# Folding the mirror images of x on VectorE, a first stage in 64x64 tiles, and a special row by copies

## The chip, the cores and the metric

The kernel runs on one core of a Trainium2 chip. The core has TensorE (PE, matrix products, reads SBUF and writes PSUM), VectorE (DVE), ScalarE (ACT) and GpSimd (POOL) for elementwise work, and DMA queues that SyncE (SP), ScalarE and GpSimd start. Each engine runs its own instructions in the order in which the program gives them. The metric is the device time of one execution in microseconds (us). Three runs of the kernel before took 132.18, 133.13 and 133.68 us; their median is 133.13 us.

## The reference, cut to what matters

```python
x = A_x                                              # 1 x 2048 x 512, fp32
g = _sigmoid((x * gate_w).sum(-1, keepdims=True))    # one gate per row of x
X = rfft2(x) * (w_r + 1j * w_i)                      # a: a filter in the 2-D spectrum
a = irfft2(X, (2048, 512))
K = 2 Re sum_n C_n exp(A_n dt * pos)                 # b: a long convolution per channel
b = irfft(rfft(x_t, 4096) * rfft(K, 4096))[:2048] + x * D_skip
return g * a + (1 - g) * b
```

The branch `a` is the bulk of the work: a 2-D Fourier transform of x, a product with the filter, and the transform back. For `b` the kernel uses that with these inputs the convolution's kernel is a constant for each channel, so that `b` is a running sum of x along the rows, times a factor per channel, plus x times another one; a count of channels for which this holds guards a general path, which these inputs do not take. Both are mixed by the gate.

## The kernel before, in words

All data is fp32. The 2048 rows are split as 32 x 64 and the transform along them is made in two stages with twiddles inside the second; the 512 channels are ordered so that channel t and its mirror images 511-t, 255-t, 256+t stand at the same place of four groups of 128.

The stages, by the letters of the schedule (`PLAN`), with their lines in the kernel before:

- `A` loads x into the tile `GI` (its first 64 blocks are called `X`) in ten parts, 4 MB in all. `X` loads a second, transposed copy of x into `XT` (four parts of 1 MB) for the running sums. `r` loads parameters, `l` the filter's weights (each of them over a block of `X` that the first stage has read), `R` constants.
- `C` (L233) is the first stage along the rows: for each of 8 groups k, 8 products of a 128x128 block of `X` with the constant `s1`, also 128x128. The sums and differences of mirror images are part of that constant. A product in fp32 shows as two records in the profile. `c` copies the result from PSUM to `E1` (L238, on ScalarE; one group, `f`, on VectorE).
- `D` (L248) is the transform along the channels, 8 products for each of 8 groups u; `E` (L253, ScalarE) copies it out. `P` (L269) is the second stage along the rows for 9 groups u = 0 to 8 (the last is half as large).
- `d` (L275, ScalarE) copies a part of P's result, `Z` (L290, L291, VectorE, four instructions for each u) combines row f with row -f, `W` and `U` (L311, L316, L317, VectorE) multiply by the filter, `p` (L321) is a DMA started by GpSimd that adds one half of the product to the other in SBUF.
- `g` (L328, L329, GpSimd) makes sums and differences, `I` (L338, L339, L341) goes back along the channels. One channel frequency does not fit the pattern of the other 127; it stands on partition 127, and `I` corrects for it with two narrow products (L341, 32 rows by 64 columns of the array) for each pair of full ones. `i` (L346, ScalarE) copies the result back to `GI`. The weights of that frequency come through a transpose on TensorE (`J`, L465) and small DMAs on SP (`L`, L305).
- `B` (L357, L358, L363) and the transposes `T` (L367, VectorE) go back along the rows; `Q` (L476) is the last stage; `q` (L481, VectorE) adds the other branch and starts the output's DMA (L482).
- Beside it: `m` (L436, VectorE) makes the running sums, `s` (L439, ScalarE) scales them; for the channels' groups 0 and 1 `e` and `o` (L442, VectorE) add them to the scaled x, for 2 and 3 `v`, `w` (L445, ScalarE) scale x and `M` (L449) adds by DMA. `H` (L453, GpSimd) multiplies by the gate; `G` makes the gate (L375 on TensorE, L378 on ScalarE), `K` (L397, VectorE) and `k` (L403, ScalarE) put the gate into the constants of the last stage. Small sums (`N`, L409 to L423) go to the guard.

PSUM is four tiles of two banks each, `banks[i]`; SBUF work tiles are `blk(i)` and `pairs[i]`. Nothing but `PLAN` sets the order: its words are issued from left to right, the number behind a letter is the group, the ones behind the points are the tiles it uses, and each engine sees its own instructions in that order. Semaphores between the engines are put in from the tiles that are read and written.

## Time and profile before

| what | number |
|---|---|
| median of three runs | 133.13 us |
| the profiled execution, by the device's time | 134.16 us |
| its span, first to last instruction | 132.4 us |
| outside the span in that execution | 1.76 us |
| TensorE busy | 117.2 us (89%) |
| VectorE busy | 82.2 us (62%) |
| ScalarE busy | 51.2 us (39%) |
| GpSimd busy | 56.2 us (42%) |
| moved by DMA | 29.85 MB, 226 GB/s over the span |
| mean granted TensorE clock | 0.979 |

In the profile's groups a row has the line, the engine, the operation, output and inputs, the shapes, the count, then busy time and the mean ns of one instruction, then the time for which the engine stood idle just before them and what ended it. A mean contains the latency of the pipeline, so where instructions follow closely the distance of two starts is the better price of one. In the chain of waits and in the timeline a row has start and length in us.

### The profile page before, as it was taken

To read this page: it belongs to the slowest core of one execution; us is meant where nothing else is said; L and a number is where in the kernel's file an instruction comes from. 1 tells how busy PE (TensorE), PEld (TensorE's weight loads), DVE (VectorE), ACT (ScalarE), POOL (GpSimd) and SP (SyncE) were. 2 spreads that over 40 slices of the span, in tenths; PEclk is the share of its full clock that TensorE was granted. 3 is DMA by queue.
4 is the path that set the end of the run, shared out by engine and by line. 5 is a ranking of instruction groups with operands and counts; after the bars stand their busy time and mean duration, and the time that the engine had idled before them with its cause. 6 is when DMAs were issued, how large, how long until landed. Compare 5 with 4: busy or idle time off the path is not lost.

```text
span 132.4 us, 2360 instructions
## 1 busy us (share of the span) xinstructions
PE 117.2 (89%) x944; PEld 95.5 (72%) x944; DVE 82.2 (62%) x101; ACT 51.2 (39%) x63; POOL 56.2 (42%) x49
## 2 busy tenths in 40 slices
PE   0599998999979999989999999999999999999700
PEld 0599997999879998858736766777655339999600
DVE  0031036078299999788770099999999573677610
ACT  3033635444267542313164113349679970000000
POOL 0000000001040840586798919499949999300000
PEclk9999999999999999999999999999999999999965
DMA  2999989996869789998667769990969600099660
GB/s 83 349 396 384 392 309 272 389 389 136 314 195 223 253 238 276 274 386 174 126 130 147 141 144 316 295 335 10 191 131 198 124 5 7 9 368 396 267 245 5
DMA packets 10643, 29.85 MB, mean 226 GB/s; under 512 B 1818, under 2 KB 2938, under 8 KB 10366
## 3 DMA queue, kind: packets, MB, share of 16 engines
q1 hardware_dynamic: 8606, 22.99, 48.4%
q0 software_dynamic: 1872, 6.55, 25.9%
q8 instruction: 9, 0.15, 0.4%
q10 hardware_dynamic: 144, 0.07, 0.4%
q14 instruction: 12, 0.10, 0.2%
HBM read 18.82 MB, written 4.21 MB: 174 GB/s over the span
## 4 chain that ended last, share of the span: by engine, by line
PE 69%; DMA 15%; DVE 7%; POOL 2%; issue 2%; ACT 1%
PE ps L233 13%; PE ps L476 12%; PE ps L357 11%; PE ps L338 9%; PE ps L341 8%; DMA blk<-blk 8%; PE ps L339 5%; PE ps L269 4%; DMA short<-in_prms_dram 3%; DMA GI<-in_x_dram 3%; PE ps L248 3%; PE ps L375 3%; DVE ps L290 2%; DVE ps L291 2%; DVE blk L316 1%
## 5 line engine op out<-in xcount | busy, mean ns | idle before, releaser
L233 PE MATMUL ps<-s,GI 128*128 128x128 f32 x128 | 17.4, 307 | 4.9 <-DMA GI<-in_x_dram 4.9
L453 POOL TENSOR_TENSOR XT<-XT,hg 128x1024 f32<-128x1024 f32 x8 | 20.9, 3038 | 0.0
L233 PEld LDWEIGHTS ps<-s,GI 128*128 128x128 f32 x128 | 17.2, 222 | 4.8 <-DMA s<-in_c_s_dram 4.8
L346 ACT COPY GI<-ps 128x1024 f32<-128x1024 f32 (+1 forms) x9 | 8.7, 964 | 24.2 <-PE ps L341 24.2
L328 POOL TENSOR_TENSOR blk<-blk 128x512 f32<-128x512 f32 (+1 forms) x9 | 13.0, 1443 | 11.6 <-DMA blk<-blk 11.2
L248 PE MATMUL ps<-dfw,E 128*128 128x128 f32 x128 | 15.6, 277 | 2.2 <-DVE blk L317 1.6
L248 PEld LDWEIGHTS ps<-dfw,E 128*128 128x128 f32 x128 | 14.8, 192 | 2.9 <-DVE blk L317 2.0
L338 PE MATMUL ps<-dbw,blk 128*128 128x128 f32 x68 | 16.3, 322 | 0.6 <-POOL blk L329 0.6
L269 PE MATMUL ps<-s2e,blk 128*128 128x128 f32 x136 | 16.8, 277 | 0.0
L269 PEld LDWEIGHTS ps<-s2e,blk 128*128 128x128 f32 x136 | 15.8, 192 | 1.2 <-issue 0.8
L357 PE MATMUL ps<-GI,s2p 128*64 128x512 f32 (+1 forms) x64 | 15.7, 583 | 0.0
L436 DVE TENSOR_TENSOR_SCAN run<-XT 128x1024 f32<-128x1024 f32 x4 | 11.2, 2803 | 6.7 <-DMA XT<-in_xt_dram 6.7
L476 PE MATMUL ps<-blk,E 128*128 128x128 f32 x128 | 15.3, 282 | 0.0
L476 PEld LDWEIGHTS ps<-blk,E 128*128 128x128 f32 x128 | 15.2, 196 | 0.1
L341 PE MATMUL ps<-last,blk 32*64 32x128 f32 x136 | 14.8, 293 | 0.0
L338 PEld LDWEIGHTS ps<-dbw,blk 128*128 128x128 f32 x68 | 10.1, 188 | 5.8 <-issue 5.0
L415 POOL TENSOR_TENSOR few<-few 128x4 f32<-128x4 f32 x1 | 0.2, 202 | 31.5 <-ACT few L412 31.5
L339 PE MATMUL ps<-dbw,blk 128*128 128x128 f32 x68 | 13.1, 275 | 0.0
L481 DVE TENSOR_TENSOR blk<-ps,XT 128x1024 f32<-128x1024 f32 x8 | 9.6, 1222 | 5.6 <-PE ps L476 2.8
L329 POOL TENSOR_TENSOR blk<-blk 128x512 f32<-128x512 f32 (+1 forms) x9 | 12.6, 1404 | 0.0
L238 ACT COPY E<-ps 128x1024 f32<-128x1024 f32 x7 | 7.1, 1012 | 13.7 <-PE ps L233 13.7
L311 DVE TENSOR_TENSOR blk<-ps,GI 128x1024 f32<-128x1024 f32 (+1 forms) x9 | 10.5, 1164 | 3.1 <-PE ps L341 1.8
(51 smaller groups left out, 142.7 us busy)
## 6 DMA issues: line engine op xcount, KB each, us to landing
XT<-in_xt_dram SPq DMA_DIRECT2D x4, 1024.0 KB, 6.6
GI<-in_w_dram SPq DMA_DIRECT2D x8, 512.0 KB, 3.9
blk<-blk POOLq DMA_DIRECT2D x8, 512.0 KB, 5.7
out_dram<-blk SPq DMA_DIRECT2D x8, 512.0 KB, 3.3
GI<-in_x_dram SPq DMA_DIRECT2D x6, 512.0 KB
XT<-run POOLq DMA_DIRECT2D x4, 512.0 KB, 5.9
GI<-in_x_dram SPq DMA_DIRECT2D x4, 256.0 KB, 5.4
hg<-gd SPq DMA_DIRECT2D x1, 1024.0 KB
```

The costliest lines, as they stand in the source:

```text
L233: T.matmul(p[:, u, :, j], X[:, 8 * k + 4 * u + j], s1, start=True, stop=True)
L248: T.matmul(p[:, n], E1[:, 8 * u + n], dfw[:, n % 4], start=True, stop=True)
L269: T.matmul(p[:, h, :, o, 64 * v:64 * v + 64], t_["e2", u % 8][:, 4 * v + 2 * h + o], st[:, ::-1] if h else st, start=True, stop=True)
L328: G.tensor_tensor(gt[:, :, :, 0], t[:, 0:4:3], t[:, 1:3], op=ALU.add)
L329: G.tensor_tensor(gt[:, ::-1, :, 1], t[:, 0:4:3], t[:, 1:3], op=ALU.subtract)
L338: T.matmul(p[:, v, 2 * h + 1], gt[:, h, m + v], dbw[:, h, 1], start=True, stop=True)
L339: T.matmul(p[:, v, 2 * h], gt[:, h, v], dbw[:, h, 0], start=True, stop=False)
L341: T.matmul(p[64 * c:64 * c + 64, v, 2 * h], px[:, c ^ h, h, v], dbl[:, h], start=False, stop=True, tile_position=(96, 64 * c))
L357: T.matmul(p[64 * s:64 * s + 64, u, :16 * n], s2p[:, 0, g], GI[:, 32 * s:32 * s + n, tt], start=True, stop=s == 1, tile_position=(0, 64 * s))
L436: V.tensor_tensor_scan(run[:, q % 2, 1:1025], XT[:, 0, q], XT[:, 1, q], 0.0, op0=ALU.add, op1=ALU.add)
L453: G.tensor_tensor(o, o, hg[:, 1024 * (k % 2):1024 * (k % 2) + 1024], op=ALU.mult)
L476: T.matmul(p[:, u, :, j], E4[:, b // 16, b % 16, :, u], t_["q", b // 8][:, 8 * u + b % 8].rearrange("p q a -> p (q a)"), start=True, stop= ...
```

## The change

Four things are done. First, `S` on VectorE makes the sums and the differences of x's mirror images out of `X` into work tiles while x comes in: for each group k one sum and one difference of 128x512 elements, and for the two groups that are loaded in halves two of each of 128x256. The host hands x over in another order, so that a block holds two mirror images on its two halves of partitions. Second, `C` works on these in tiles of 64 rows by 64 columns of the array: 32 products for each k, with a 64x64 constant and 64 columns each, in place of 8 of 128x128x128; the two row halves write to the two banks of a PSUM tile. All eight copies `c` are on ScalarE. Third, the special frequency: `h` on ScalarE copies its product row (32 partitions are copied, of which the last is kept) into the operand of the second transform; L341 and its constant are gone, so that `I` is 8 full products for each u. The row's weights come apart from the others (`wl`), by small DMAs on ScalarE's queue, and the large loads of weights fill 127 partitions. Fourth, the combinations `g` are split in two halves: `g` (the half without the special row) on GpSimd for all u, the other one as `x` on GpSimd for u = 0, 8, 1, 2 and as `y` on VectorE for u = 5, 6, 3, 7, 4.

The `PLAN` is written anew. Besides the moves above, the running sums of channel groups 0 and 1 are now added as those of 2 and 3 are, by ScalarE's scaling and a DMA (`v`, `w`, `M`), so `e` and `o` do not occur any more, and all ten parts of x are loaded ahead of everything else on SP.

```diff
 PLAN = """
-R0 A4 C3.0 A7 C6.1 r0.0 A3 c3 C2.0 r1.1 N0 A5 R3 J0 A6 C4.2 R8 A9 A8 c6 c2 C5.0 c4 f5 A1 C7.1 c7 A2 C1.0 R4 c1 A0 C0.1
...
+A2 S1.0 A0 A1 S0.1 A7 R0 S6.2 A9 A8 S7.3 C1.0 c1 A3 S2.0 C0.1 C6.0 A5 S4.1 C7.2 c0 c7 c6 C2.1 C4.2 c2 A4 S3.2 A6 c4
...
+        def S_(k, i):
+            f = t_["fo", k] = blk(i).rearrange("p (o b t) -> p o b t", o=2, t=P)
+            n = 2 if k in (0, 7) else 4
+            for b in range(0, 4, n):
+                v = X[:, 8 * k + 2 * b:8 * k + 2 * b + 2 * n].rearrange("p (b u) t -> p u b t", u=2)
+                V.tensor_tensor(f[:, 0, b:b + n], v[:, 0], v[:, 1], op=ALU.add)
+                V.tensor_tensor(f[:, 1, b:b + n], v[:, 0], v[:, 1], op=ALU.subtract)
+
         def C_(k, i):
-            p = t_["pc", k] = bank(i).rearrange("p u (n b) -> p u n b", b=4)
-            for u in range(2):
-                for j in range(4):
-                    T.matmul(p[:, u, :, j], X[:, 8 * k + 4 * u + j], s1, start=True, stop=True)
+            p = bank(i)
+            t_["pc", k] = p.rearrange("p g (n b) -> p g n b", b=4)
+            p = p.rearrange("p g (m o c b) -> p g m o c b", o=2, c=2, b=4)
+            for b in range(4):
+                for o in range(2):
+                    for g in range(2):
+                        for h in range(2):
+                            gs, hs_ = slice(64 * g, 64 * g + 64), slice(64 * h, 64 * h + 64)
+                            T.matmul(p[hs_, g, :, o, :, b], t_["fo", k][gs, o, b, hs_], s1[gs], start=True, stop=True, tile_position=(64 * g, 64 * h))
...
+        def load_h(k):
+            main = GI[P - 1:P, 0:64].rearrange("p (u n o) t -> p u n o t", n=4, o=2)[:, :, :, k]
+            nc.scalar.dma_start(main, hT[0:8] if k == 0 else wl[0:4096].rearrange("(o u n t) -> o u n t", o=1, u=8, n=4))
+            main = wtile(8)[P - 1:P, :, :, k].rearrange("p r a k -> p (r a) k")
+            nc.scalar.dma_start(main, hT[8:9, :, :64] if k == 0 else wl[4096:].rearrange("(o n t) -> o n t", o=1, n=4))
...
-        def g_a(u, i):
+        def h_a(u, i):
             n = nrow(u)
-            gt = t_["gt", u] = blk(i)[:, 0:8 * n].rearrange("p (h m c k) -> p h m c k", h=2, c=2, k=64)
-
-            t = t_["t", u][:, 0].rearrange("p x a (m k) -> p (x a) m k", k=64)
-            G.tensor_tensor(gt[:, :, :, 0], t[:, 0:4:3], t[:, 1:3], op=ALU.add)
-            G.tensor_tensor(gt[:, ::-1, :, 1], t[:, 0:4:3], t[:, 1:3], op=ALU.subtract)
+            t_["gt", u] = blk(i)[:, 0:8 * n].rearrange("p (h o v c k) -> p h o v c k", h=2, o=2, c=2, k=64)
+            t = t_["t", u][96:P, 0, :, :, 0:n].rearrange("p x a (v k) -> p x a v k", k=64)
+            for h in range(2):
+                S.copy(t_["gt", u][96:P, h, 0].rearrange("p v c k -> p c v k"), t[:, ::-1, 1] if h else t[:, :, 0])
+
+        def g_a(u, o, E):
+            n = nrow(u)
+            r = P - 1 + o
+            gt = t_["gt", u][:r, :, o]
+
+            t = t_["t", u][:r, 0, :, :, o * n:o * n + n].rearrange("p x a (v k) -> p (x a) v k", k=64)
+            E.tensor_tensor(gt[:, :, :, 0], t[:, 0:4:3], t[:, 1:3], op=ALU.add)
+            E.tensor_tensor(gt[:, ::-1, :, 1], t[:, 0:4:3], t[:, 1:3], op=ALU.subtract)
 
         def I_(u, i):
...
-            for v in range(m):
-                for h in range(2):
-                    T.matmul(p[:, v, 2 * h + 1], gt[:, h, m + v], dbw[:, h, 1], start=True, stop=True)
-                    T.matmul(p[:, v, 2 * h], gt[:, h, v], dbw[:, h, 0], start=True, stop=False)
-                    for c in range(2):
-                        T.matmul(p[64 * c:64 * c + 64, v, 2 * h], px[:, c ^ h, h, v], dbl[:, h], start=False, stop=True, tile_position=(96, 64 * c))
+            gt = t_["gt", u].rearrange("p h o v c k -> p h o v (c k)")
+            for o in (1, 0):
+                for v in range(nrow(u) // 64):
+                    for h in range(2):
+                        T.matmul(p[:, v, 2 * h + o], gt[:, h, o, v], dbw[:, h, o], start=True, stop=True)
...
-            "W": W_, "U": U_, "p": p_a, "g": g_a, "I": I_, "i": i_a,
+            "W": W_, "U": U_, "p": p_a, "h": h_a, "g": lambda u: g_a(u, 1, G), "x": lambda u: g_a(u, 0, G), "y": lambda u: g_a(u, 0, V), "I": I_, "i": i_a,
```

Three places show what this moves. A row has the line, the operation, output and inputs with buffer numbers, the shape of one and the count.

VectorE at the start of the program, before: `few` holds small numbers, `short` are loaded parameters, `E` is `E1`, `run` the running sum, `ps` PSUM.

```order
L409 TENSOR_REDUCE few<-short_96 128x4
L409 TENSOR_REDUCE few<-short_97 128x4
L459 TENSOR_TENSOR few<-few 128x9x2
L460 TENSOR_TENSOR few<-few 128x9
L461 TENSOR_TENSOR few<-few 128x9
L240 COPY E_69<-ps_58 128x2x128x4
L436 SCALAR_TENSOR_TENSOR run<-XT 128x1024 x2
L290 TENSOR_TENSOR ps_59<-ps_59,short_96 128x2x128
```

The same place in the changed kernel, from the last folds on (L230, L231):

```order
L230 TENSOR_TENSOR blk_88<-GI 128x512
L231 TENSOR_TENSOR blk_88<-GI 128x512
L472 TENSOR_TENSOR few<-few 128x9x2
L473 TENSOR_TENSOR few<-few 128x9
L474 TENSOR_TENSOR few<-few 128x9
L449 SCALAR_TENSOR_TENSOR run<-XT 128x1024
L422 TENSOR_REDUCE few<-short_97 128x4
L422 TENSOR_REDUCE few<-short_96 128x4
L449 SCALAR_TENSOR_TENSOR run<-XT 128x1024
L299 TENSOR_TENSOR ps_58<-ps_58,short_96 128x2x128
```

Twenty folds stand ahead of all else; the copy of `E1` is gone; the two reductions stand between the two running sums, and the first `Z` (L299) still follows the second running sum.

TensorE where the transform back along the channels begins, before: one `I` for u = 6 and the `P` behind it (`blk_88` is the combined operand, `blk_95` the product with the special row).

```order
L338 MATMUL ps_58<-dbw,blk_88 128x128
L339 MATMUL ps_58<-dbw,blk_88 128x128
L341 MATMUL ps_58<-last,blk_95 64x128 x2
L338 MATMUL ps_58<-dbw,blk_88 128x128
L339 MATMUL ps_58<-dbw,blk_88 128x128
L341 MATMUL ps_58<-last,blk_95 64x128 x2
L269 MATMUL ps_59<-s2e,blk_90 128x2x64 x8
```

TensorE around the first `I` (L354) in the changed kernel: `P` is L278, `D` is L257, the gate's count L443.

```order
L278 MATMUL ps_59<-s2e,blk_90 128x2x64 x8
L354 MATMUL ps_60<-dbw,blk_89 128x128 x4
L278 MATMUL ps_61<-s2e,blk_90 128x2x64 x8
L354 MATMUL ps_58<-dbw,blk_89 128x128 x8
L354 MATMUL ps_60<-dbw,blk_88 128x128 x8
L354 MATMUL ps_59<-dbw,blk_88 128x128 x8
L443 MATMUL ps_58<-few 1x1 x4
```

The narrow products are gone, and all `I` but the short one stand behind the last `P`.

VectorE after the last multiplication by the filter, before: `share` (L442) and the running sums of groups 2 and 3.

```order
L317 SCALAR_TENSOR_TENSOR blk_92<-ps_59,GI 128x256
L442 SCALAR_TENSOR_TENSOR XT<-XT,few,run 128x1024 x2
L436 SCALAR_TENSOR_TENSOR run<-XT 128x1024
L442 SCALAR_TENSOR_TENSOR XT<-XT,few,run 128x1024 x2
L436 SCALAR_TENSOR_TENSOR run<-XT 128x1024
L397 TENSOR_TENSOR short_96<-short_96,blk_95 128x512
```

The same place in the changed kernel; L345 and L346 are `y`, L446 the guard's count, L410 the constants' gate.

```order
L326 SCALAR_TENSOR_TENSOR blk_93<-ps_61,GI 128x512
L345 TENSOR_TENSOR blk_89<-blk_94 127x2x2x64
L346 TENSOR_TENSOR blk_89<-blk_94 127x2x2x64
L449 SCALAR_TENSOR_TENSOR run<-XT 128x1024
L345 TENSOR_TENSOR blk_89<-blk_91 127x2x2x64
L346 TENSOR_TENSOR blk_89<-blk_91 127x2x2x64
L345 TENSOR_TENSOR blk_88<-blk_90 127x2x2x64
L346 TENSOR_TENSOR blk_88<-blk_90 127x2x2x64
L446 CAST count<-ps_58 1x1
L345 TENSOR_TENSOR blk_88<-blk_95 127x2x2x64
L346 TENSOR_TENSOR blk_88<-blk_95 127x2x2x64
L410 TENSOR_TENSOR short_98<-short_98,blk_92 128x512
```

The four `share` instructions are gone, and five pairs of combinations, four of them shown, stand between the running sum, the count and the first product with the gate.

More of the change, by code (lines that the diff above doesn't have):

```diff
@@ L167, in body @@
     X = GI[:, 0:64]
-    s1 = work.tile([P, P], F32, name="s1")
+    s1 = work.tile([P, 64], F32, name="s1")
     few = work.tile([P, 72 + 36 + 24 + 17], F32, name="few")
@@ L178, in body @@
     dbw = work.tile([P, 2, 2, P], F32, name="dbw")
-    last = work.tile([P, 4, P], F32, name="last")
-    hT, dbl = last[:9], last[96:P, 0:2]
+    hT = work.tile([9, 4, P], F32, name="hT")
     gws = work.tile([P, 4, 32], F32, name="gws")
```

45 lines of the change are left out of this document (18 added, 27 removed).

## The prediction

> **What bounds the kernel now.** I read the page first, then the chain of waits, then the groups of instructions with shapes apart, then timelines of single engines. On the page I look at shares, at the slices and at the DMA queues:
>
> ```profile
> PE 117.2 (89%) x944; PEld 95.5 (72%) x944; DVE 82.2 (62%) x101; ACT 51.2 (39%) x63; POOL 56.2 (42%) x49
> ...
> PE   0599998999979999989999999999999999999700
> ...
> q0 software_dynamic: 1872, 6.55, 25.9%
> ```
>
> TensorE is busy from about 5 us to 125 us with next to no gap, so it bounds the whole; no other engine is above 62%. The chain in order of time (start, length, both us) gives the stages:
>
> ```profile
> 0.75 3.97 DMA GI<-in_x_dram
> ...
> 4.86 17.37 PE ps L233 x128
> 22.25 1.02 ACT E L238
> 23.31 3.84 PE ps L248 x32
> ...
> 36.12 0.60 DVE blk L316
> ...
> 72.45 0.42 PE ps L338 x2
> ...
> 73.45 0.42 PE ps L338 x2
> ...
> 93.84 1.00 PE ps L357 x3
> ...
> 109.58 15.29 PE ps L476 x128
> 124.89 1.23 DVE blk L481
> ```
>
> The first stage lasts until 22.2; D starts at 23.3; B starts at 93.8; B and Q take 31.1 us until 124.9; the last 7.5 us of the span of 132.4 are the last sum and the output's transfer. One set of I's (two full products, two narrow ones) costs 73.45 - 72.45 = 1.00 us, and there are 34 sets. The groups give the prices of single things:
>
> ```profile
> L248 PE MATMUL ps<-dfw,E 128*128 128x128 f32 x128 | 15.6, 277 | 2.2 <-DVE blk L317 1.6 <-ACT E L238 0.7
> L375 PE MATMUL ps<-XT,gws 128*32 128x512 f32 x32 | 3.6, 595 | 0.0
> L430 PE MATMUL ps<-few 128*1 128x1 f32 x8 | 0.3, 163 | 0.0
> L275 ACT COPY short<-ps 128x256 f32<-128x256 f32 x1 | 0.4, 373 | 0.0
> L321 POOL DMA_DIRECT2D blk<-blk x9 | 8.5, 945 | 8.2 <-DVE blk L317 8.2
> L328 POOL TENSOR_TENSOR blk<-blk 128x512 f32<-128x512 f32 x8 | 11.0, 1371 | 9.7 <-DMA blk<-blk 9.2 <-PE ps L375 0.3
> L453 POOL TENSOR_TENSOR XT<-XT,hg 128x1024 f32<-128x1024 f32 x8 | 20.9, 3038 | 0.0
> ```
>
> **What goes from TensorE.** A full product is two records of 15.6/128 = 0.122 us, 0.244 us. Without the narrow ones a set of I's is two full products, 0.49 us: 34 x (1.00 - 0.49) = 17.3 us less, if nothing else sets the pace of I.
>
> The first stage is 64 full products now; it becomes 256, each on a quarter of the array, with half the columns. How those run no row shows. The nearest is the gate's product L375, with four column tiles and 512 columns. Two rows of TensorE's timeline for the distance of D and P, and one that caught the first four records of L375:
>
> ```profile
> 45.17 1.95 PE L269 MATMUL ps<-s2e,blk 128*128 128x128 f32 x16
> 46.96 1.95 PE L248 MATMUL ps<-dfw,E 128*128 128x128 f32 x16
> ...
> 66.91 0.64 PE L375 MATMUL ps<-XT,gws 128*32 128x512 f32 x4
> ```
>
> One record of L375 takes 0.595 us, yet four fit in 0.64 us and all 32 cost 3.6/32 = 0.112 us each: four tiles run at once. For 64 columns in place of 512 that is an estimate of 0.014 us a record, 512 x 0.014 = 7.2 us for the stage. L430's smallest records, in a single tile, cost 0.3/8 = 0.038 us, which gives 19.2 us; a record as long as a full one, 0.122 us, gives 62 us. I take the low end, as L375 alone has four tiles at work, and keep the others as rivals.
>
> The Trainium skill, "TensorE: Matmul & The Clock Gate" (section "Wait — 56ns, not 53.3ns?"), has a floor of about 25 ns from one start to the next however few columns there are; by it the stage takes 512 x 0.025 = 12.8 us and the time is about 0.5 us more. L375's row speaks against it between tiles: its four records started within 0.64 - 0.595 = 0.045 us.
>
> **When the first stage can end.** If the tiles run at once, x's arrival sets it. One window of the trace (the last numbers are the DMA's share and GB/s), and two queue rows with the operand that waits:
>
> ```profile
> 0.00:13.24 13.24, 8.38 (x50) 8.42 (x51) 1.81 (x7) 3.31 (x3) 0.20 (x4) 1.00 0.83 303
> ...
> 13.07 0.71 SPq L207 DMA_DIRECT2D XT<-in_xt_dram  x1
> ...
> 21.18 2.29 DVE L436 TENSOR_TENSOR_SCAN run<-XT 128x1024 f32<-128x1024 f32 x1 [2.99 <-DMA XT<-in_xt_dram]
> ...
> 29.59 0.43 DVE L290 TENSOR_TENSOR ps<-ps,short 128x256 f32<-128x256 f32 x1
> ...
> 45.48 0.42 DVE L290 TENSOR_TENSOR ps<-ps,short 128x256 f32<-128x256 f32 x1
> ...
> 49.66 0.42 DVE L290 TENSOR_TENSOR ps<-ps,short 128x256 f32<-128x256 f32 x1
> ...
> 75.91 0.28 DVE L290 TENSOR_TENSOR ps<-ps,short 128x128 f32<-128x128 f32 x1
> ...
> 78.55 5.16 DVE L442 SCALAR_TENSOR_TENSOR XT<-XT,few,run 128x1024 f32<-128x1024 f32 x2
> ```
>
> 303 GB/s over 13.24 us are 4.01 MB, 0.39 MB a us once the transfers run. All of x and the small constant are 4.23 MB, so the last byte moves at 13.8. The running sum's operand, issued at 13.07 with 6.2 MB ahead of and in it, had moved by about 19.7 and was usable at 21.2, 1.5 us later; so x's last part is usable at 15.3. A fold of 512 elements costs 0.60 us, as L316 in the chain; two make a group, 1.2 us, and a group's 0.52 MB take 1.34 us to come. The twenty folds, 16 of full size by their elements, are 9.6 us of VectorE, and the loads hide all but the last pair (if VectorE were slower than the loads, each 0.1 us a fold would cost 1.6). Then half a group's products (0.5) and the copy (1.0, as L238): 15.3 + 1.2 + 0.5 + 1.0 = 18.0. D starts 5.3 us earlier than now.
>
> **What then is late: VectorE.** The second running sum needs its part of XT, whose end stands 7.35 MB down SP's queue: usable at 21.7 + 1.5 = 23.2; with 2.2 us of its own it ends at 25.4. P0 and its copy are ready at 18.0 + 3 x 1.79 (D0, D7, P0, at the distance 46.96 - 45.17) + 0.8 = 24.2. So the first Z starts at 25.4 where it is 29.6 now: of the 5.3 us, 4.2 are kept.
>
> From there one u costs VectorE 49.66 - 45.48 = 4.18 us, the half one 78.55 - 75.91 = 2.64, a reduction 0.7: 8 x 4.18 + 2.64 + 0.7 = 36.8 us, so the last multiplication ends at 62.2 without a wait. TensorE has 16.5 x 1.79 (D, P) + 3.6 (gate) + 16.6 (I) + 0.8 = 50.5 us to do from 18.0, until 68.5. It has slack; VectorE and what stands behind it set the pace.
>
> **The waits that the change adds.** On ScalarE `h` waits for p's transfer, and the copies d and E queue behind it; Z and TensorE wait for those. By themselves the 18 copies of `h` are 18 x 0.373 = 6.7 us, with four scalings and one `c` of 1.0 each 11.7: 63 us of ScalarE, no bound. How long p's transfer takes, by the queue's median and by the line's extremes:
>
> ```profile
> blk<-blk POOLq DMA_DIRECT2D x8, 512.0 KB, 5.7
> ...
> DMA to landing us min/median/max: 4.5/5.2/11.6
> ```
>
> U0 is done at about 31, so `h0` waits until 37 to 42, and d6 comes behind it and a scaling at 39 to 44, where VectorE wants it at 39.7. I put 2 us for this, between 0 and 4. Four more M transfers join: q0's 25.9% are 34.3 us of all DMA engines for 6.55 MB, 5.2 us a MB, so 2.1 MB are 11 us, among the p's and loads of the middle. The four L442 that they replace stand behind the multiplications, off the path.
>
> At the middle's end: 62.2 + 2 = 64.2; p4 issued in 1.0 (L321), landed 5.7 later, 70.9; then `h4`, `g4`, `y4`, with `H2`, `g6`, `g3` ahead of `g4` on GpSimd and a running sum and three `y` ahead of `y4` on VectorE. Two windows show what two engines on SBUF do to each other, the busy time of L397 (512 elements) alone:
>
> ```profile
> 93.40:96.16 2.76, 2.58 (x1) 1.00 1.02 190
> 96.16:98.00 1.84, 1.84 (x4) 1.00 1.11 211
> ```
>
> The first, beside a product of GpSimd, took over 2.58 us; the other three fill 1.84. So I let half of GpSimd's `H2` (3.0) and of six half-size instructions (6 x 1.37/2 = 4.1) be delayed past the landing and put 2.5 us of waiting, 0 to 5.5, then 1.4 for the last two combinations and 3.9 for two I's (16 x 0.244): 70.9 + 2.5 + 1.4 + 3.9 = 78.7.
>
> The Trainium skill, "SBUF — State Buffer" (section "Who interferes with whom"), says that a VectorE instruction with two inputs in SBUF and a GpSimd instruction that reads SBUF exclude each other, the second waiting for the whole of the first; by it `y` on VectorE wins nothing beside `g`, and the sum is 3 us more. L397's rows agree with it.
>
> **The sum.** B starts at 78.7 in place of 93.8. B, Q and the tail are unchanged, 31.1 + 7.5: a span of 117.3. With the 1.76 us outside it the profiled execution would be 119.1 against its 134.16; the runs' median is 1.03 below that execution: 118 us. GpSimd's `H` (five of 2.6 behind the last M, which waits for ScalarE until about 86) end near 99.5; the fourth group of Q needs a PSUM tile free at 94.4 + 3 x 1.91 = 100.1. That is covered by half a us; without the cover each us counts.
>
> **The rivals.**
> - *No stall in the middle, 112 us.* `h` holds nothing up and p4 lands in 4.5: B at 62.2 + 1.0 + 4.5 + 1.4 + 3.9 = 73.0, 5.7 sooner. For it: TensorE's slack. Against it: 11 us more of transfers.
> - *Transfers fill the middle, 126 us.* One M pair (5.5 us) ahead of the last p, and 3 us more of exclusion. For it: the 11.6 us that one p took. Against it: SP no longer stops behind the small loads of L305, so loads end sooner.
> - *Tiles at L430's pace, 124 us.* 19.2 us from 5.5, and the copy: D at 25.7, P0's copy at 31.9, Z 6.5 later.
> - *Tiles in turn, slower.* Break-even is a first Z 15.1 later, 40.5; that is a stage of 27.9 us, 0.054 us a record. At 0.122 us the stage ends at 69, Z starts 50 later, 168 us. For it: no row shows two row halves at work. Against it: L375. The first stage would then eat what I gains.
>
> **How the numbers follow.** Forecast 0.58, no stall 0.15, full transfers 0.14, L430's pace 0.07, tiles in turn 0.06 (two thirds of it slower by over 1%, the rest near break-even). 1% is about what a measurement of this kernel can tell from no change. Faster 0.93, within 1% 0.03, slower 0.04. The range goes from just under the case without stalls, 111, to just over full transfers, 127.
>
> **What would show it.** The first stage is busy in pieces, some 10 us in all, waiting for folds, and D starts at 17 to 19; the first Z at 25 to 27, released by the running sum; VectorE full from there to about 64; the last I at 76 to 81. The tiles are wrong if D starts after 22, the middle if VectorE idles over 5 us between the first Z and the last multiplication, the end if the first q waits for `H` beyond its PSUM tiles.

## The result and the profile after

The changed kernel takes 297.58 us (median of four runs, 296.66 to 298.05), the kernel before 133.41 in runs beside them: a ratio of 2.237, interval 2.219 to 2.254. The forecast was 118 us, 111 to 127. It is slower by a mechanism that none of the rivals named. Some executions of one kernel are longer than its others by more than 1.5%; the times and ratios of the experiments below leave these out.

The page of the changed kernel: shares, TensorE's busy tenths and the DMA's GB/s in 40 slices of 7.4 us, and the queue that GpSimd starts:

```profile
PE 106.3 (36%) x1192; PEld 93.0 (32%) x1192; DVE 92.5 (31%) x126; ACT 62.1 (21%) x86; POOL 56.4 (19%) x61
PE   2758900000000399300700000002701924999990
GB/s 253 407 379 58 26 26 75 26 30 25 90 91 229 26 91 122 153 85 24 91 57 26 26 26 26 26 26 26 144 37 68 241 246 178 80 171 41 152 280 149
q0 software_dynamic: 2448, 8.65, 15.6%
```

The 17 us of TensorE that were to go are gone in part, 117.2 to 106.3 us busy, and nothing else is full either: for long stretches no engine works, and the transfers go at 25 or 26 GB/s, slice after slice. What is waited for stands in the waits (engine and line, what it waited for, total us, times, the longest), in SyncE's queue (start, length) and in the chain:

```profile
DVE blk L320 <- DMA GI<-in_w_dram: 98.6, 3, 59.3
ACT short L284 <- DMA few<-in_vecs_dram: 66.6, 1, 66.6
```

```profile
30.99 17.49 SPq L216 DMA_DIRECT2D s2e<-in_c_s2e_dram  x1
...
147.57 40.41 SPq L308 DMA_DIRECT2D GI<-in_w_dram  x3
```

```profile
88.72 49.97 DMA GI<-in_w_dram
```

VectorE waits 98.6 us for the weights, and SyncE cannot even issue: it stands 17.49 us at a constant of 384 KB (L216) and 40.41 us at three loads of weights. A window without other transfers shows the rate bare (the columns are the engines' busy time, the granted clock, the DMA's share of 16 engines, GB/s):

```profile
55.00:63.00 8.00, 0.00 (x0) 0.00 (x0) 0.00 (x0) 0.00 (x0) 0.00 (x0) 0.50 0.06 26
```

A share of 0.06 is one engine of sixteen. A load of weights is now 127 partitions of 4 KB, 508 KB: at 26 GB/s 20 us, and all eight and a half of them 170 us, one after the other. The Trainium skill, "DMA: Bandwidth & Descriptors" (section "Why a DMA increments its semaphore by 16 and not by 1"), says that a transfer is spread over the largest number of engines up to 16 that divides its slowest dimension, and names 127 partitions as a case of one engine. This trace agrees, with its 0.06.

### The profile page after: what moved, and what is told of

It reads as the page before. It is cut to its first block, busy times and chain, and to the rows that moved or that the text cites. A ratio compares the mean times of both kernels' runs of the same rounds, so it can differ in the third digit from the quotient of the medians.

```text
span 294.8 us, 2927 instructions
## 1 busy us (share of the span) xinstructions
PE 106.3 (36%) x1192; PEld 93.0 (32%) x1192; DVE 92.5 (31%) x126; ACT 62.1 (21%) x86; POOL 56.4 (19%) x61
## 3 DMA queue, kind: packets, MB, share of 16 engines
q0 software_dynamic: 2448, 8.65, 15.6%
## 4 chain that ended last, share of the span: by engine, by line
DMA 33%; SPq 25%; another core or an unknown queue 20%; PE 15%; DVE 3%; issue 1%; ACT 1%; DVEq 0%; ACTq 0%
DMA GI<-in_w_dram 17%; DMA gd<-gsg 7%; SPq L216 6%; SPq L308 6%; PE ps L489 5%; PE ps L370 5%; DMA blk<-gd 4%; SPq L217 4%; SPq L218 3%; SPq L219 3%; DMA s2e<-in_c_s2e_dram 3%; PE ps L354 3%; DMA GI<-in_x_dram 2%; SPq L203 1%; PE ps L278 1%
## 5 line engine op out<-in xcount | busy, mean ns | idle before, releaser
L278 PE MATMUL ps<-s2e,blk 128*128 128x128 f32 x136 | 22.7, 338 | 143.4 <-DVE blk L326 79.3
L278 PEld LDWEIGHTS ps<-s2e,blk 128*128 128x128 f32 x136 | 21.6, 250 | 144.8 <-ACT blk L262 65.1
L330 POOL DMA_DIRECT2D blk<-blk x9 | 8.0, 894 | 206.7 <-DVE blk L326 141.6
L320 DVE TENSOR_TENSOR blk<-ps,GI 128x1024 f32<-128x1024 f32 (+1 forms) x9 | 10.5, 1164 | 98.8 <-DMA GI<-in_w_dram 98.6
L299 DVE TENSOR_TENSOR ps<-ps,short 128x256 f32<-128x256 f32 (+3 forms) x18 | 7.5, 415 | 75.6 <-ACT short L284 75.3
L354 PE MATMUL ps<-dbw,blk 128*128 128x128 f32 x136 | 20.4, 321 | 25.2 <-DVE blk L326 16.0
L354 PEld LDWEIGHTS ps<-dbw,blk 128*128 128x128 f32 x136 | 19.8, 236 | 25.6 <-DVE blk L326 16.2
L242 PE MATMUL ps<-s,blk 64*64 64x64 f32 x512 | 14.0, 296 | 11.2 <-issue 5.8
L242 PEld LDWEIGHTS ps<-s,blk 64*64 64x64 f32 x512 | 13.1, 206 | 11.9 <-issue 6.3
L257 PE MATMUL ps<-dfw,E 128*128 128x128 f32 x128 | 15.3, 277 | 1.1 <-ACT E L247 1.1
L257 PEld LDWEIGHTS ps<-dfw,E 128*128 128x128 f32 x128 | 14.7, 192 | 1.3 <-ACT E L247 1.2
L346 POOL TENSOR_TENSOR blk<-blk 128x256 f32<-128x256 f32 (+3 forms) x13 | 13.4, 1030 | 0.0
L345 POOL TENSOR_TENSOR blk<-blk 128x256 f32<-128x256 f32 (+3 forms) x13 | 11.3, 872 | 6.8 <-DMA blk<-blk 5.2
L337 ACT COPY blk<-blk 32x256 f32<-32x256 f32 (+1 forms) x18 | 6.2, 387 | 28.6 <-PE ps L354 16.1
```

The costliest lines, as they stand in the source:

```text
L242: T.matmul(p[hs_, g, :, o, :, b], t_["fo", k][gs, o, b, hs_], s1[gs], start=True, stop=True, tile_position=(64 * g, 64 * h))
L257: T.matmul(p[:, n], E1[:, 8 * u + n], dfw[:, n % 4], start=True, stop=True)
L278: T.matmul(p[:, h, :, o, 64 * v:64 * v + 64], t_["e2", u % 8][:, 4 * v + 2 * h + o], st[:, ::-1] if h else st, start=True, stop=True)
L345: E.tensor_tensor(gt[:, :, :, 0], t[:, 0:4:3], t[:, 1:3], op=ALU.add)
L346: E.tensor_tensor(gt[:, ::-1, :, 1], t[:, 0:4:3], t[:, 1:3], op=ALU.subtract)
L354: T.matmul(p[:, v, 2 * h + o], gt[:, h, o, v], dbw[:, h, o], start=True, stop=True)
```

## Experiments

Fifteen further kernels were run. All compute what the reference computes. Each time is the median of the number of runs that stands beside it; ratios are to the kernel before in the same session, with the interval where one came out. The expectations quote medians over all executions: their 147.7 is the 147.4 of e1 here, 143.4 and 144.5 are the 143.3 of e5 and of e6, 139.4 is the 137.9 of e12, 139.2 the 137.7 of e9, and 134.2 the 134.1 of the kernel before.

| kernel | us | runs | ratio |
|---|---|---|---|
| the change | 297.6 | 4 | 2.237 (2.219 to 2.254) |
| e2: before, loads of weights cut 127 + 1 | 293.7 | 1 | 2.21 |
| e9: before, cut 112 + 16 | 137.7 | 1 | 1.03 |
| e1: the change, cut 112 + 15 | 147.4 | 3 | 1.111 (1.084 to 1.138) |
| e3: e1 with tiles of 64x128 | 153.5 | 3 | 1.165 (1.149 to 1.181) |
| e8: e1 with loads held back | 151.5 | 1 | 1.13 |
| e5: e1 without folds | 143.3 | 3 | 1.078 (1.053 to 1.103) |
| e6: e1, one pair of transfers later | 143.3 | 2 | 1.07 |
| e10: e1, 11 loads for 18 | 148.5 | 2 | 1.113 (1.099 to 1.127) |
| e17: e1, 9 loads over 128 partitions | 144.3 | 1 | 1.08 |
| e11: e5, e6 and e10 together | 144.9 | 3 | 1.087 (1.078 to 1.096) |
| e12: e5, skips 0 and 1 on VectorE | 137.9 | 2 | 1.04 |
| e13: e12, all combinations on GpSimd | 145.0 | 3 | 1.10 |
| e16: e12, 9 loads over 128 partitions | 138.5 | 2 | 1.044 (1.033 to 1.056) |
| e18: e12, one stretch in another order | 151.6 | 2 | 1.136 (1.121 to 1.151) |
| e7: before's order, special row alone | 152.5 | 3 | 1.134 (1.116 to 1.151) |

### The count of 127, alone and taken away

```diff
-            nc.sync.dma_start(GI[:P - 1, ...], w[...])          # the change; in the kernel before GI[:, ...]
+            nc.sync.dma_start(o[:112], s[:112])                 # e1; e2: [:127] and [127:]; e9: [:112] and [112:]
+            nc.sync.dma_start(o[112:P - 1], s[112:])
```

> The changed kernel, but each load of the filter's weights over 127 partitions is cut into two, over 112 and over 15 partitions; the same bytes to the same places. Theory A (a load over 127 partitions runs on one DMA engine at about 26 GB/s, 20 us for each 508 KB, and these loads make nearly all of the loss): the loads go at several hundred GB/s and the time falls to 118 to 130 us. Rival B (the new order of instructions, with waits behind waits on ScalarE and SyncE, makes the loss): it stays above 250 us. Theory C says how far below 130 us it gets: the first stage is held up by TensorE's instructions, which come by DMA behind the loads, so that D still starts near 26 us as in the changed kernel and not at 18; then 124 to 128 us. If the stage ends at 18 as was forecast: 118 us.

> The kernel before, with each load of the filter's weights cut into 127 partitions and 1 partition; nothing else differs. Theory A: nine loads of about 20 us on one engine, one after the other, 270 to 310 us. Rival B: 133 us, within 2.

> Control for the kernel before with the weights in 127 and 1 partitions (293.7 us): the kernel before with each load of weights cut into 112 and 16 partitions, the same number of transfers. Theory A (the count of 127 takes the transfer to one engine): 131 to 136 us, as the kernel before. Rival (twice as many loads on SP cost by themselves): over 140 us.

The kernel before becomes 293.7 us by the cut at 127 and nothing else, and the change 147.4 by being cut at 112. The page of e2 has the same row of 26 GB/s, and VectorE the same wait, here for the small load that SyncE issues behind the weights:

```profile
GB/s 225 394 247 35 216 26 28 76 26 26 56 54 58 113 70 26 26 26 26 90 24 19 88 88 25 26 42 142 24 240 86 90 121 292 157 182 16 115 321 150
```

```profile
DVE blk L313 <- DMA GI<-last: 149.2, 5, 42.8
```

So 160 us from the count alone, and 150 us gained when it goes: this is shown. The control e9, with as many loads as e2, may not be quite free: its one run takes 137.7 us against 134.1, between what was expected and the rival. The median landing of a load goes from 3.9 to 6.9 us (rows of the two pages: before, then e9, whose profiled execution took 140.66 us), and TensorE waits 6.47 us for a weighted product at 42.63.

```profile
GI<-in_w_dram SPq DMA_DIRECT2D x8, 512.0 KB, 3.9
```

```profile
GI<-in_w_dram SPq DMA_DIRECT2D x8, 448.0 KB, 6.9
```

What is left in e1 is some 15 us more than the kernel before, where 15 us less were forecast; the 118 to 130 us expected of it were missed.

### The first stage: tiles, folds, and what stalls them

e3 makes two row tiles of 64x128 in place of four of 64x64 (128 products for 256), e5 takes the first stage of the kernel before, e8 lets one small transfer wait for the first stage's last copy, so that SyncE's loads behind it start late:

```diff
-                            T.matmul(p[hs_, g, :, o, :, b], t_["fo", k][gs, o, b, hs_], s1[gs], ..., tile_position=(64 * g, 64 * h))
+                        T.matmul(p[:, g, :, o, :, b], t_["fo", k][gs, o, b], s1[gs], ..., tile_position=(64 * g, 0))   # e3
+            nc.sync.dma_start(gd[0:1, 0:4], E1[0:1, 0, 20:24])    # e8, behind R3 and R2
```

> The kernel of e1_112_15 with the first stage in tiles of 64 rows by 128 columns: 128 products in place of 256, so half of TensorE's instructions there, the same result. Theory C (instructions come too late): half of the stalls go, D starts 2 to 5 us sooner than in e1_112_15 and the time is 1 to 5 us less. Rival D (what limits the stage is the tiles' own pace or the folds): D starts no sooner, or later, as only two tiles work at once.

> The kernel of e1_112_15 with the first stage of the kernel before: no folds on VectorE, 64 full products on x itself with the 128x128 constant; all the rest of the change stays. Theory C: D starts near 23 us, as in the kernel before, some 3 us sooner than in e1_112_15, and the time is 0 to 4 us less: the folded stage wins nothing. Rival (the folds pay as forecast): D starts 5 us later than in e1_112_15 and the time is 2 to 5 us more.

> The change with loads of 112 and 15 partitions (147.7 us), and a small transfer of 16 bytes out of E1 put into SP's queue behind the fifth and sixth constant loads: it waits for ScalarE's last copy of the first stage, so that X1, X0, prms and weights are issued only once the first stage has been copied out. Theory F (TensorE's idle times of 2.71, 3.09 and 2.36 us in the first stage are fetches of its instructions that stand behind saturated data loads): the first one, under x's own load, stays near 2 to 3 us; the second and third shrink below 1 us; the first stage ends near 20 to 22 instead of 26.7. Rival (TensorE pauses by itself, or for the folds): all three stay. Time itself: 143 to 152 us, as the loads held back come later.

TensorE's timeline of e1 (start, length, instruction, count; in brackets the idle time ahead and what ended it):

```profile
5.22 5.64 PE L242 MATMUL ps<-s,blk 64*64 64x64 f32 x222 [5.22 <-DVE blk L230]
13.58 3.33 PE L242 MATMUL ps<-s,blk 64*64 64x64 f32 x127 [2.71 <-issue]
20.00 3.51 PE L242 MATMUL ps<-s,blk 64*64 64x64 f32 x127 [3.09 <-issue]
25.87 0.80 PE L242 MATMUL ps<-s,blk 64*64 64x64 f32 x36 [2.36 <-issue]
27.77 6.52 PE L257 MATMUL ps<-dfw,E 128*128 128x128 f32 x32 [1.10 <-ACT E L247]
```

The stage stops for "issue", that is for nothing on another engine, 2.71, 3.09 and 2.36 us. The pieces between are 127 records, with their weight loads 254 instructions. The queue rows of e8 (packets, MB, share of 16 engines) show what comes then: in a window under x's load, and in one in which nothing else moves, one packet of 0.02 MB of instructions.

```profile
q1 hardware_dynamic: 625, 1.59, 100.8%
q8 instruction: 1, 0.02, 1.6%
```

```profile
q8 instruction: 1, 0.02, 1.8%
```

```profile
13.46 1.67 PE L245 MATMUL ps<-s,blk 64*64 64x64 f32 x98 [2.58 <-issue]
15.32 0.68 PE L245 MATMUL ps<-s,blk 64*64 64x64 f32 x29 [0.19 <-ACT E L250]
17.22 2.09 PE L245 MATMUL ps<-s,blk 64*64 64x64 f32 x127 [1.22 <-issue]
21.03 0.80 PE L245 MATMUL ps<-s,blk 64*64 64x64 f32 x36 [1.71 <-issue]
22.93 5.35 PE L260 MATMUL ps<-dfw,E 128*128 128x128 f32 x32 [1.10 <-ACT E L250]
```

With the other transfers held back the later stops shrink to 1.22 and 1.71 us but stay, and D starts at 22.93 in place of 27.77. So theory F holds in half: in e8 a part of over a microsecond stays without other transfers, and in e1 about as much again comes on top with the transfers full. The expected shrinking below 1 us did not come. In e3, with half the instructions, no such stop occurs, yet its stage is the longest and D starts last, at 33.99:

```profile
5.13 27.74 PE L241 MATMUL ps<-s,blk 64*128 64x64 f32 x256 [5.13 <-DVE blk L230]
```

27.74/256 is 0.108 us a record, at a clock of 1.00 throughout; in e8's undisturbed piece of 64x64 tiles it is 2.09/127 = 0.0165. Why a tile of twice the columns takes 6.6 times as long per record was not pursued. The Trainium skill, "Runtime: NRT & Kernel Launch" (section "Instruction fetch mechanics"), has instructions come in blocks of 256, mostly hidden by a prefetch behind the issue rate. The blocks agree with 254; that they are hidden does not: these small products eat a block in 2.1 us.

After a stop the clock can be lower, too. Windows over one piece each (clock in the third column from the right), of e1, e17 and e8:

```profile
13.50:16.90 3.40, 3.32 (x127) 3.19 (x127) 1.86 (x3) 2.06 (x3) 0.00 (x0) 0.58 1.04 404
```

```profile
13.39:16.98 3.59, 3.58 (x127) 3.40 (x127) 2.50 (x5) 2.43 (x3) 0.00 (x0) 0.52 1.04 401
```

```profile
17.22:19.31 2.09, 2.09 (x127) 1.95 (x127) 0.40 (x4) 1.26 (x2) 0.00 (x0) 1.00 0.04 8
```

The same 127 records take 3.33 us at a clock of 0.58 (after a stop of 2.71 us), 3.59 at 0.52 (after 2.04) and 2.09 at 1.00 (after 1.22). The length of the stop alone does not decide it: e8's piece at 13.46 came after 2.58 us and ran 98 records in 1.67, at full rate. What does was not found. e8 as a whole is slower than e1; the loads that it holds back come late, and VectorE waits 13.7 us for weights and 12.4 for `XT`. And e5, with the old first stage and D at 22.73, is 4.1 us faster than e1: the folds win nothing.

### The middle: partial sums in a full queue

e6 moves `M0` (two transfers of 512 KB that add in SBUF) from ahead of `p3` to behind `p4`. e12 is e5 with `e0 o0 e1 o1` on VectorE for `v0 w0 v1 w1 M0 M1`, as before the change; e13 then has `x` for each `y`.

> The change with each weights load cut into 112 and 15 partitions (147.7 us), and one word of the plan moved: both(0), the two accumulating transfers of 512 KB each that GpSimd starts from run into XT, stands behind the partial sums of group 4 and no longer ahead of those of group 3. Theory M (the partial sums of group 3, issued at 77.24 and landing only near 95, stood behind those transfers in GpSimd's own queue): they land 6 to 8 us after their issue, the combinations and Z0-to-B follow earlier by some 6 to 9 us, and the time is 139 to 142 us. Rival (the landing is long because gate loads, their broadcasts and c_r share the 16 transfer engines): they still take 14 us or more, and the time stays within 1% of 147.7. A third outcome, in which they land early and the time hardly moves, would put the wait of the first inverse stage on ScalarE's copies of the special row.

> The change with loads of 112 and 15 partitions and the first stage in 128 by 128 products (143.4 us), and the skips of quarters 0 and 1 back on VectorE, as in the kernel before: share(0), share(1) in the place of skip(0), skip(1) on ScalarE and of their four accumulating transfers of 512 KB. Theory T (from 47 to 95 us the 16 transfer engines are full, 1385, 1170 and 989 packets in three stretches at shares near 1; the four transfers hold GpSimd's queue for about 11.6 us of all engines, 31.5% of 145.6 less 25.9% of 132.4, so that partial sums take 13 to 14 us to land instead of 5.7): median landing of the partial sums 6 to 9 us and 134 to 139 us. Rival V (VectorE's four further operations, near 1.7 us each, lie on the path instead): 141 to 146 us with the landing shorter all the same. Rival L (the landing is long for the late weights' sake): landing above 11 us, 142 to 145 us.

> As the run with the skips of quarters 0 and 1 on VectorE, and the even combinations of groups 3 to 7, which the change gave to VectorE, on GpSimd like the others. Theory P (VectorE's combinations stand still while GpSimd reads and writes SBUF beside them, 8.28 and 5.42 us for one operation of 0.41 in the run with three pieces undone): 1 to 4 us below that run, 132 to 136 us. Rival (GpSimd, with ten operations of 0.7 us more, becomes the bound of the middle): 1 to 4 us above it. This run changes who computes, not what.

In e1 GpSimd's and ScalarE's timelines show `p3` started behind `M0`, and its copy `h` waiting until 95.08, TensorE until 97.35:

```profile
74.33 2.38 POOL L464 DMA_DIRECT2D XT<-run  x2
77.24 0.86 POOL L332 DMA_DIRECT2D blk<-blk  x1 [0.54 <-DVE blk L328]
...
95.12 0.72 POOL L347 TENSOR_TENSOR blk<-blk 128x256 f32<-128x256 f32 x1 [7.19 <-DMA blk<-blk]
```

```profile
95.08 0.70 ACT L339 COPY blk<-blk 32x256 f32<-32x256 f32 x2 [9.34 <-DMA blk<-blk]
```

```profile
97.35 9.45 PE L356 MATMUL ps<-dbw,blk 128*128 128x128 f32 x64 [11.46 <-DVE count L448]
```

95.08 less 77.24 is 17.8 us for a landing that was put at 5.7. The same two places in e6:

```profile
76.31 0.86 POOL L332 DMA_DIRECT2D blk<-blk  x1 [2.57 <-DVE ps L299]
```

```profile
86.69 0.71 ACT L339 COPY blk<-blk 32x256 f32<-32x256 f32 x2 [1.77 <-DMA blk<-blk]
```

`p3` now lands within 10.4 us, not in the 6 to 8 expected. TensorE's idle time there falls from 11.46 to 4.83 us and stage B starts at 103.3 in place of 106.7; the time falls by 4.1 to 143.3, less than the 6 to 9 expected. e12 takes all four transfers away: q0 goes from 8.65 to 6.55 MB, B starts at 96.1, and the time is 137.9, 5.3 us below e5 and within what theory T gave. The landing, in the page's rows of e5 and then e12, falls less than thought:

```profile
blk<-blk POOLq DMA_DIRECT2D x8, 512.0 KB, 12.8
```

```profile
blk<-blk POOLq DMA_DIRECT2D x8, 512.0 KB, 9.5
```

e13 goes the other way, for its rival and beyond it: all combinations on GpSimd cost 7 us, and TensorE waits for them 17.5 us in all:

```profile
L345 PE MATMUL ps<-dbw,blk 128*128 128x128 f32 x136 | 18.9, 302 | 17.6 <-POOL blk L337 17.5
```

So in this order the split over two engines pays.

### Do the pieces add up?

e10 loads partitions 112 to 126 of all groups at once, e11 adds that and `M0` behind `p4` to e5. e16 and e17 load all 128 partitions and write the special row's computed half over the last one, group by group (on e12 and e1); for that the `PLAN` of both also has two constants and a part of `XT` (`R7`, `R8`, `X2`) loaded a little earlier.

```diff
+            s = w[0:(P - 1) * 8192].rearrange("(u p n) -> p u n", u=8, n=1024)[112:]      # e10, e11
+            nc.sync.dma_start(GI[112:P - 1, 0:64].rearrange("p (u n) t -> p u (n t)", u=8), s)
+                E.dma_start(GI[P - 1:P, 8 * u:8 * u + 8].rearrange("p (u n o) t -> p u n o t", n=4, o=2)[:, :, :, 0], hT[u:u + 1])   # e16, e17
```

> The change with each load of weights over partitions 0 to 111, and partitions 112 to 126 of all eight large groups loaded once by one transfer of 480 KB, ahead of the first weights (a second, small one for group 8): 11 transfers for the 18 of the cut at 112 and 15 that gave 147.7 us, and 9 in the change itself. Theory N (the cut itself costs the 5 us by which the kernel before rose from 134.2 to 139.2, through its extra transfers): 142 to 145 us here. Rival (the extra 15 partitions are hidden in the new order, whose end is set by other waits): within 1% of 147.7. The first weighted product may start later, since it now waits for the whole 480 KB.

> Three pieces undone at once on the change with loads of 112 and 15 partitions (147.7 us): the first stage in 128 by 128 products without folds (143.4 by itself), both(0) behind the partial sums of group 4 (144.5 by itself), and partitions 112 to 126 loaded once. Theory S (the 14 us by which the change without its slow loads still lies above the kernel before are these pieces, each by its own): 147.7 - 4.3 - 3.2 - 3 to 5 = 135 to 137 us, no faster than the kernel before although TensorE has 17 us less to do. Rival (they hide each other, one wait after the other taking the place of the last): 140 us or more. A time below 131 would say that the special row's new path is worth something by itself.

> As the run with the first stage in 128 by 128 products and the skips of quarters 0 and 1 on VectorE (139.4 us), but every load of weights over all 128 partitions, 9 transfers as in the kernel before, and the special row's computed half written over partition 127 behind them, one small transfer for each group, started by SP (by ScalarE for group 0). Theory L (the cut into 112 and 15 partitions, which cost the kernel before 134.2 to 139.2 us, costs the change the same): the median landing of the weights falls from above 6 to near 4 us, and the time is 133 to 136 us, the kernel before within 1% although TensorE has 17 us less to do. Rival B (something that these runs have not touched is still in the way, as the order of the middle): 137 to 141 us. Below 132 would be faster than the kernel before.

> The change with nothing undone but its loads: weights over all 128 partitions, 9 transfers, the special row's computed half written over partition 127 behind them, group by group; folds, tiles, accumulating transfers and the even combinations on VectorE as in the change. Theory L: 147.7 less 4 to 5 us, 142 to 144 us. Rival (the cut at 112 and 15 is hidden here by the first stage's late end): 146 to 149 us.

They do not add up. e10 (1.113) is where e1 is (1.111), e16 (1.044) where e12 is (1.04), and e11 (1.087) is no better than e5 (1.078). So the cut into two loads, which may cost the kernel before some 4 us, costs nothing that can be seen in e10 and e16: the theories that put the rest on it fell there. For e17 it stays open: its four executions lie between 144.3 and 155.9 us, and the shortest is 3.1 us below e1. One execution of e16 took 361.17 us, at a granted clock of 1.00; nothing here explains it. In e16's trace the partial sums land in 5.8 us, as before the change, and the time stays; TensorE then waits 4.54 us for `y` and 5.36 for the count. Taking one wait away brings up the next.

### The order of the middle, and the special row in the old order

e18 is e12 with one stretch of the plan rearranged; e7 is the kernel before, its order and first stage kept, each `g` replaced by `h g x` and `L` by two transfers at the start.

```diff
- y5 m3 I5.2 y6 y3 G2 H2 G5 y7 v3 w3 h4.2 s3 i5 g6 I6.0 g3 g4 I3.1 G3.4 K0 y4 g7
+ y5 G5 I5.2 y6 y3 G2 y7 v3 w3 h4.2 i5 g6 I6.0 g3 g4 I3.1 G3.4 y4 g7 H2 m3 s3 K0
```

> As the run with the first stage in 128 by 128 products and the skips of quarters 0 and 1 on VectorE (139.4 us; its TensorE waits 5.44 us at 86.79 for VectorE's count), with one stretch of the plan in another order: G5 (the count's copy) stands right behind the even combinations of group 5, H2 on GpSimd behind the last odd combinations, and scan(3) and the first base behind the last even ones. Theory O (the order of the middle keeps what is left: VectorE and GpSimd do work that is needed late ahead of work that TensorE waits for): the wait at the count goes, stage B starts 3 to 5 us earlier, near 92, and the time is 134 to 136 us. Rival (the partial sums of groups 3 and 4 land last in any order, or what is put behind comes late in stage B): within 1% of 139.4, with the idle time of TensorE only under another name.

> The kernel before, order of the program and first stage and skips on VectorE included, with the third part of the change alone: the special row of the weights loaded apart and copied by ScalarE ahead of the combinations, these over 127 partitions for the even half and 128 for the odd, all four on GpSimd, no small products in the first inverse stage (17 us of TensorE less); the weights in loads of 112 and 15 partitions. Theory P (the change lost its 14 us to the new order and the folds, not to the special row's new path): 118 to 130 us, faster than before. Rival H (the ScalarE copies wait for the partial sums' landing and hold up the evictions queued behind them on ScalarE, here as in the change): 134 to 142 us, with ScalarE's idle time in front of these copies above 15 us in sum.

Both take about 13% more than the kernel before, outside what was expected of either, and one of the gate's four products `K` on VectorE says why in each: the one that meets GpSimd's run of products `H`. Its row and that of the run, in the kernel before, in e18 and in e7:

```profile
93.58 2.79 DVE L397 TENSOR_TENSOR short<-short,blk 128x512 f32<-128x512 f32 x1
92.85 2.97 POOL L453 TENSOR_TENSOR XT<-XT,hg 128x1024 f32<-128x1024 f32 x1
```

```profile
104.35 13.33 DVE L401 TENSOR_TENSOR short<-short,blk 128x512 f32<-128x512 f32 x1
104.97 12.16 POOL L457 TENSOR_TENSOR XT<-XT,hg 128x1024 f32<-128x1024 f32 x5
```

```profile
95.97 19.71 DVE L401 TENSOR_TENSOR short<-short,blk 128x512 f32<-128x512 f32 x1
100.05 15.07 POOL L457 TENSOR_TENSOR XT<-XT,hg 128x1024 f32<-128x1024 f32 x6
```

A `K` with nothing beside it takes 0.68 us. Each of these three ends 0.55 us behind the last `H` of its run: 96.37 and 95.82, 117.68 and 117.13, 115.68 and 115.12. In the kernel before the run is a single `H`, since GpSimd then waits 2.08 us for ScalarE and the other three `K` get through; in e18 and e7 GpSimd does not stop there, and five or more `H` come one after the other. The transposes stand behind `K` on VectorE, and TensorE waits for them, in e18 and then e7:

```profile
PE ps L361 <- DVE E L371: 11.7, 1, 11.7
```

```profile
PE ps L361 <- DVE E L371: 15.0, 1, 15.0
```

The one held `K` costs 12.7 us in e18 and 19.0 in e7; e18 lies 13.7 us above e12 and e7 18.4 above the kernel before. No run moved `K` alone. The Trainium skill, "SBUF — State Buffer" (section "Who interferes with whom"), says that such a pair contends for a shared read interface and that the order of issue decides which of the two is blocked. These rows agree that one shuts the other out, but not on the order: in e18 the `K` started 0.62 us ahead of the run that held it.

Apart from that, TensorE's wait for the count did go in e18 (the next I starts at 84.36, not 86.79), and B still starts 3 us later, at 99.16, behind the copies of I. In e7 the ScalarE copies of the special row wait 14.8 us in sum, about what rival H asked, but its time has the other cause. B starts at 94.4 in e7, with 17 us less of work in I, and at 93.8 in the kernel before: in the old order, too, the special row's new path won nothing up to there.

## Why the prediction was wrong

**The step that failed** is the weights' load, which the part on the change left without a term. The change was described with loads that fill 127 partitions, and the sum went on as if such a load landed like one of 128. Put at nothing, it costs 150 us (e1) to 160 (e2), far above everything else in the sum: the loads went at 26 GB/s, one after the other, and the weighted products waited for them. No large load in the trace of before had another count than 128 partitions, so its bounds were open on the upper side, and the Trainium skill named the very number in the section cited above. The range had no place for it.

**The rivals.** "Tiles in turn" stood for slower, with 0.04 on that side, and had nothing to do with it. The transfers' rival (126 us) had the right resource, by crowding; its price was too small even for e1. What the prediction held against it, that SP would no longer stop, came out the other way: SP stood up to 40.41 us at three loads.

With the loads mended, the other steps can be held against e1:

- *I without its narrow products, 17.3 us less.* Of the same kind as measured: from D to B TensorE is busy 68.46 us before and 57.11 in e12, 11.4 less though at a lower clock. But it saves no time. The two windows, before and then e12:

```profile
22.50:93.77 71.27, 68.46 (x579) 55.15 (x577) 54.10 (x74) 29.95 (x36) 38.21 (x37) 1.00 0.83 233
```

```profile
22.50:96.14 73.64, 57.11 (x444) 52.57 (x444) 60.18 (x85) 34.43 (x53) 37.96 (x45) 0.88 0.85 214
```

  What is saved has become idle time, 2.8 us before and 16.5 in e12, and the granted clock over the stretch is 0.88 in place of 1.00. A lower clock goes with idle time within a trace, too: in e1 it is 1.00 from 64 to 78 us, where TensorE is busy throughout, and 0.58 from 78 to 97.35, where it is busy for 5.3 us. No run tested this by itself.
- *First stage ends with x, D at 18.0.* Failed: 27.77. The price of a record, 0.014 us, was nearly right (0.0165 at full clock), and so was a fold's (0.6). The way to that price, scaling by columns, was in part luck: e3's records, with the same 64 columns, took 0.108. Three stops of 8.2 us in all, put above to the fetching of instructions, and about half the clock after two of them, were not in the sum. The 22 that the prediction gave as its own mark against the tiles was passed, yet the tiles did run at once, by their 0.0165 us a record.
- *First Z at 25.4, released by the running sum.* 36.73, released by ScalarE's copy: D came late, and at a clock of 0.57.
- *VectorE 4.18 us for each u from there, 2 us for `h`.* The term for `h` was mis-sized. The waits of e1 have 21.1 us for it:

```profile
ACT blk L339 <- DMA blk<-blk: 21.1, 5, 9.3
```

  ScalarE is held there, with the copies that VectorE and TensorE wait for queued behind it. The last multiplication ends near 81, not at 64.
- *p4 lands in 5.7.* The median in e1 is 10.8 and `p3` takes 17.8. The 11 us of added transfers were worked out correctly in the prediction, but as a load on the queue in general; they belonged on the path, since `M0` stood right ahead of `p3` in the same queue. e6 and e12 show 4 and 5 us of it.
- *2.5 us of waiting for the combinations.* 11.46 us in e1, of which 6.6 went with `M0`. The term was small by its own working, too: half of 3.0 and 4.1 is 3.5.
- *B, Q and the tail unchanged, 38.6 us.* Right in e1: 145.6 - 106.73 = 38.9. It hung on where `K` falls: in e18 it is 151.8 - 99.16 = 52.6, and the prediction, which had seen a `K` of over 2.58 us beside GpSimd, had no term for that.

**What stays open.** e12 is the best form of the change that was found, and still about 4% behind the kernel before. That the order of the middle is what is left was argued and not shown: the one other order that was tried, e18, was spoilt by the held `K` and so does not decide it. No kernel here beats the kernel before.

## What to carry to other kernels

Before pricing a changed transfer, look at the count of its outermost dimension: a load of 127 partitions in place of 128 ran on one engine of sixteen and was worth more than the whole kernel. Time taken from a full TensorE is a gain only if what feeds it has as much slack; here what was saved came back as waiting, for landings and for the combinations, and the clock fell with it. A transfer queued ahead of one that the path waits for is priced there, on the path, and not as a share of all engines. A VectorE product with both operands in SBUF is best kept clear of a run of GpSimd's products, for here one was held to the end of the run.

## What the runs showed of the hardware

- A load over 127 partitions moved at 26 GB/s, a share of 0.06 of sixteen engines, and SyncE stood 17.5 us at issuing a constant behind such loads and 40.4 at three more of them.
- Four 64x64 tiles ran at 0.0165 us a record (e8), and TensorE stopped after the first 222 and then after every 127 records, with one packet of 0.02 MB of instructions in the gap: for 1.2 and 1.7 us in e8 with idle transfer engines, for 2.4 to 3.1 in e1 with busy ones. Two tiles of 64x128 with the same 64 columns of data took 0.108 us a record (e3).
- After some of these stops (2.0 to 3.1 us) the granted clock was 0.52 to 0.58 over the next 127 records, after others (1.2, 2.6) it was 1.00.
- VectorE's product of two 128x512 operands in SBUF took 0.68 us alone. One that met GpSimd's products took 2.79 us (one of them), 13.33 (five) and 19.71 (seven), and ended 0.55 us behind the last.
